# An attention and FFN block on one core: VectorE's exp as one quadratic per octave, and 256-query sets

## The chip, the cores and the metric

The kernel runs on one core of a Trainium2 chip, in one launch. The metric is device time in microseconds, the median of several runs. The core has five engines with in-order queues of their own: TensorE (PE, its weight loads shown as PEld), VectorE (DVE), ScalarE (ACT), GpSimd (POOL, which does almost nothing here) and SyncE (SP), which issues the DMAs. They wait for each other by semaphores.

## The reference

One transformer block for 2048 tokens of width 512, bf16 in and out. `mod` is six vectors of 512 made from a conditioning vector; attention has 32 heads of 16.

```python
h = _layernorm(x) * (1 + ca) + sa
qkv = (h @ wqkv)                      # q, k, v: 32 heads of 16
p = _softmax(q @ k.T * 16 ** -0.5)    # per head, 2048 x 2048
x = x + ga * ((p @ v) @ wo)
h = _layernorm(x) * (1 + cb) + sb
x = x + gb * ((gelu(h @ w_gate) * (h @ w_up)) @ w_down)   # F = 1792
```

The exps of the softmax are 32 x 2048 x 2048, a million columns of 128.

## The kernel before

**Recording and planning.** The Python class `_Recorder` records every operation with the memory it reads and writes, works out the semaphore waits, and keeps an estimate of when each engine will be free. The scheduling loop `stream` (line 1218) asks these estimates which operation to put next. What it decides is the fixed order of each engine's instructions in the built program; on the chip nothing is decided any more. Every matmul is issued from line 315, every ACT operation from line 328, DVE operations from lines 332 (two tensors), 340 (tensor and scalars), 345 (multiply-add of both), 349 (copy or cast), 352 (reciprocal) and 368 and 371 (layer norm statistics).

**The stream.** Queries are split into sets (`SETS`, line 31): three of 512, one of 256, two of 128. For each set there are eight units, one for each of eight groups `qd` of four heads, called head groups here. A unit walks over all keys in rounds; a round is four items (one for each of the four heads), and an item is one PSUM bank of 512 columns of scores: 128 keys x 512 queries, or 256 keys x 256 queries, or 512 x 128. The loop of `stream` takes items in *chunks* of three banks; there are two such triples, so while ACT works on one, PE fills the other (`qk`, line 1479). ACT takes the exp of a whole chunk in one instruction, from `ps_sc` to the buffer `E`. `pv_mms` (line 1491) then multiplies a round of `E` with V into the unit's accumulator `ps_pv`; V has a 17th column of ones that gives the softmax's denominator. The first two units are interleaved while K and V are still being projected.

**Exps on DVE.** In some chunks ACT takes two of the banks and DVE the third: it writes `score * a + b`, rounded to uint16, into a quarter of `kq` (tiles named `dreg` and `mreg` in the trace). Read as bf16, these bits are a power of two with a linear mantissa, a piecewise linear exp. After four such banks, a whole round (a *quad* in the code), DVE makes four copies of the 2048 columns with the bits shifted by the constants of `SHIFT` (line 60; `shift_task`, line 1503; in the trace `mreg<-dreg` and `mreg<-mreg` 128x2048). PV takes the five versions one after the other, the shifted ones with copies of V scaled by `2 ** (-shift / 128)` (`vs`), so that the five linear pieces add up to a closer exp. The scaled V exists for keys from tile `T0` = 12 on, so only such rounds may go to DVE. A new quad is begun only under conditions (lines 1394 to 1396): DVE not far behind, a backlog under `BACK`, a free `kq` buffer, and, once the third set's units are over, a low PE `credit` (PE's allowance for side work).

**Side work.** Projections, and for each finished set the output projection (`side_wo`), the second layer norm (`ln2_steps`) and the FFN (`side_ffn`), are generators whose matmuls are put between the chunks by the credits of `plan` (line 1144); they use the one bank `ps_mi`. A set's side work runs while the next set's attention does. `FLOW` sets stream gate, up and down weights anew, 256 KB a transfer, into `wst` and `wdst`; the later sets use weights that `weight_parts` loads once. gelu is made with a tanh on ACT (`wreg<-wreg`) and four DVE operations. A unit's end (`unit_end`, line 1525) copies the accumulator to `osb`, sends the denominators by DMA to other partitions, takes the reciprocal, sends it back broadcast to `rb` and multiplies. For the last two head groups (6 and 7) of the last two sets this is done without DMA by `near_end` (line 947): an fp32 matmul with `self32` spreads the denominators, DVE takes the reciprocal and the product.

**The tail.** After the last exp, `tail` (line 1580) orders what is left: the last set's (queries 1920 to 2047) wo, layer norm and FFN (`tail_end`, `tail_last`), and what is left of the FFN of the set before it (`tail_rest`). The last set but one is queries 1792 to 1919.

**Filler.** PE gets matmuls without use (`ps_sc<-xs,ident` and `ps_mi<-xs,ident`) when it would be idle for long.

Of the kernel before, what the change touches and what calls it, by code (L numbers as in the profile page):

```python
# [6 lines left out]
ALU = mybir.AluOpType  # L7
# [23 lines left out]
SETS = ((0, 512), (512, 512), (1024, 512), (1536, 256), (1792, 128), (1920, 128))  # L31
OCOL = (0, 0, 0, 0, 256, 384)
BCOL = (0, 0, 0, 0, 0, 128)
# [7 lines left out]
T0 = 12  # L41
NK = 3
CREDIT = 2048
NS = 4
AHEAD = (30, 44)
FLOW = 3
# [4 lines left out]
BACK = 8  # L51
# [8 lines left out]
SHIFT = (26, 51, 77, 102)  # L60
SHIFT_C = float(128 * (127 - np.log2(5) - 0.0565))
# [359 lines left out]
class _Kernel(_Recorder):  # L421
# [12 lines left out]
    def alloc(self):  # L434
# [9 lines left out]
        self.tb2 = hreg[:, 0:4 * D].rearrange("p (t n) -> p t n", t=4)  # L444
# [5 lines left out]
        self.wst = [[mreg[:, 1024 * (2 * x + b):1024 * (2 * x + b) + 1024].rearrange("p (a n) -> p a n", a=NDC)  # L450
                     for b in range(2)] for x in range(2)]
# [9 lines left out]
        self.wu = [self.wst[i // 2][i % 2] for i in range(4)]  # L461
        self.wu += [dreg[:, 1024 * i:1024 * i + 1024].rearrange("p (a n) -> p a n", a=NDC) for i in range(4, 7)]
# [3 lines left out]
        self.vs = sb("vs", [P, len(SHIFT), NKT - T0, H * VW], BF16)  # L466
# [245 lines left out]
    def side_v(self, g, dc):  # L712
        mi = self.mi[:, :]

        def part(t):
            for dci in range(NDC):
                self.mm(mi[:, P * t:P * t + P], self.hT[:, dci, 512 * g + P * t:512 * g + P * t + P],
                        self.wqkv[:, dci, 1024 + P * dc:1024 + P * dc + P],
                        start=(dci == 0), stop=(dci == NDC - 1))
        for t in range(4):  # L720
            yield 512, lambda t=t: part(t)
        dst = self.vaug[:, 4 * g:4 * g + 4, VW * 8 * dc:VW * 8 * dc + VW * 8]
        self.copy("dve", dst.rearrange("p t (h c) -> p t h c", c=VW)[:, :, :, 0:DH],
                  mi.rearrange("p (t h c) -> p t h c", t=4, c=DH))
        self.done(("v", g, dc))
        if 4 * g == T0 and not self.dry:
            c = slice(VW * 8 * dc, VW * 8 * dc + VW * 8)
            self.task([lambda i=i, o=o: self.ts("dve", self.vs[:, i, :, c], self.vaug[:, T0:NKT, c], float(2.0 ** (-o / 128)),
                                                None, ALU.mult) for i, o in enumerate(SHIFT)], ("vs", dc))
        yield END  # L730
# [155 lines left out]
    def normed(self, k, i):  # L886
        return self.E[:, NSL - 1, :] if k == len(SETS) - 1 else self.tb2[:, i, :]

    def merged(self, gi):
        return MERGED[gi >= len(SETS) - 2]  # L890
# [91 lines left out]
    def side_ffn(self, gi, part=None):  # L982
# [10 lines left out]
        width = max(2, kpb)  # L993
        for a in range(0, NFC, width):
            chunks.append(range(a, min(NFC, a + width)))

        def load(x, ci):
            if flow and ci < len(chunks):
                v = (self.B_w_gate, self.B_w_up)[x].rearrange("(a p) n -> p a n", p=P)
                self.dma("sp", self.wst[x][ci % 2], v[:, :, 2 * P * ci:2 * P * ci + 2 * P], "st%d%d" % (x, ci % 2))  # L1000
# [12 lines left out]
        for h in range(2):  # L1013
            yield from self.side_t(lambda t: self.normed(gi, t), n, h,
                                   lambda dc: self.t2T[:, dc, c0:c0 + W], self.modB)

        def up(x, ci, sub):
            for s, fc in enumerate(sub):
                for dci in range(NDC):
                    if flow:  # L1020
                        lhs = self.wst[x][ci % 2][:, dci, P * (fc % 2):P * (fc % 2) + P]
# [43 lines left out]
        for i in range(3):  # L1065
            load_down(i)
        for ci in range(nch + 1):
            yield from near()
            if ci < nch:
                yield from G(ci)  # L1070
                yield from near()
                if ci >= nch - 2:
                    load_down(3 + ci - nch + 2)
            if ci >= 1:
                yield from U(ci - 1)
                if ci >= nch - 1:
                    load_down(5 + ci - nch + 1)
# [21 lines left out]
    def urgency(self, tk):  # L1099

        if tk[1] is not None and tk[1][0] in ("rec", "norm", "onorm", "stats", "rstd", "den") or tk[1] in ((("ln2", len(SETS) - 1, h) for h in range(2))):
# [3 lines left out]
        if tk[1] is None or tk[1][0] in ("st2", "ln2"):  # L1105
            return -1
        if tk[1] is None or tk[1][0] != "shift":
            return 1
        return 0 if self.plain[tk[1][1]] <= URGENT else 2
# [34 lines left out]
    def plan(self, ends, nsplit):  # L1144
# [15 lines left out]
        due = (ends[1] + 30, ends[2] + 30, ends[3] + 30, ends[4] - 20)  # L1160
        for k, e in enumerate(due):
            s0 = ends[k] + 33
            w.append((lambda k=k: self.side_wo(k), s0, min(e, s0 + 15 * SETS[k][1] // P)))
            w.append((lambda k=k: self.side_ffn(k), s0, e))
        k, s0 = len(SETS) - 2, ends[-2] - 16
# [52 lines left out]
    def stream(self):  # L1218
# [7 lines left out]
        units = [((k,), qd) + SETS[k] for k in range(4) for qd in range(8)]  # L1226
        units += [((4, 5), qd, SETS[4][0], 2 * P) for qd in range(QS)]
        units += [((k,), qd) + SETS[k] for k in (4, 5) for qd in range(QS, 8)]
# [3 lines left out]
        ends = [0] * len(SETS)  # L1232
# [13 lines left out]
        for u in units[2:]:  # L1246
            n, kpb = NKT * u[3] // 512, 512 // u[3]
            plain = list(range(T0 // kpb))
            m = len(plain) * 2 // 3
            for r in plain[:m] + list(range(len(plain), n)) + plain[m:]:  # L1250
# [13 lines left out]
        for u, r, g0 in rounds:  # L1264
# [7 lines left out]
        cand = [k for k, (u, r, g0) in enumerate(rounds)  # L1272
                if u not in units[:2] and r * (512 // u[3]) >= T0]
# [60 lines left out]
        def pv_do(x):  # L1334
# [10 lines left out]
            else:  # L1345
                q["ready"].remove((i, src))
                q["n"] -= 1
                if i:
                    self.sq_free.append(q["slots"].pop(i))
# [9 lines left out]
        while cg <= group[units[-1]]:  # L1359
            parts = early or late  # L1360
            if parts and pos >= loaded and (pos >= ends[2] + 8 if early else ("ffn", 2) in self.have):
# [15 lines left out]
            if tq is not None and tq <= t + 30:  # L1377
# [9 lines left out]
                if len(mem) == CH and "modB" in self.have and self.free["dve"] < t + 700:  # L1387
                    while quad is None and cand and last[rounds[cand[0]][0]] < pos + AHEAD[rounds[cand[0]][0][3] == 512]:
# [5 lines left out]
                    elif (not overdue and cand and self.quad_free and (pos < ends[2] or self.credit < CREDIT or (self.next_side() is None and self.waiting[0] in ("onorm", "osb"))) and rounds[cand[0]][2] < pos + 96 and self.backlog() < BACK  # L1394
                          and ("vs", rounds[cand[0]][0][1] // 2) in self.have
                          and all(k in self.have for k in self.keys(seq[rounds[cand[0]][2]]))):
                        rnd = rounds[cand.pop(0)]
                        quad = {"rnd": rnd, "j": [0, 1, 2, 3], "k": self.quad_free.pop(0), "ready": [], "n": NS + 1, "slots": {}}
                        left[rnd[0]] += NS
# [24 lines left out]
                if g is not None:  # L1424
                    kq = self.kq[quad["k"]]
                    self.ts("dve", kq[:, 512 * j:512 * j + 512].bitcast(U16), self.scp[:, s0 + n, :], 128 / OCT, SHIFT_C,
                            ALU.mult, ALU.add)
                    if not quad["j"]:
                        quad["ready"].append((0, [kq[:, 512 * x:512 * x + 512] for x in range(4)]))
                        wait.append(quad)  # L1430
                        for i in range(NS):
                            self.shift_task(quad, i)
# [39 lines left out]
        self.tail(len(SETS) - 2, len(SETS) - 1)  # L1472
# [18 lines left out]
    def pv_mms(self, rnd, acc, src, i, first, last):  # L1491
# [3 lines left out]
        for kk in range(kpb):  # L1495
            kt = r * kpb + kk
            v = self.vs[:, i - 1, kt - T0, :] if i else self.vaug[:, kt, :]
            for j in range(4):
                h = 8 * dc + 2 * j + ee
                self.mm(acc[32 * j:32 * j + VW, 0:W], v[:, VW * h:VW * h + VW], src[j][:, W * kk:W * kk + W],  # L1500
                        start=first and kk == 0, stop=last and kk == kpb - 1, tp=(0, 32 * j))

    def shift_task(self, q, i):

        def f():
            s = self.sq_free[0]
            self.ts("dve", self.sq[s].bitcast(U16), self.kq[q["k"]].bitcast(U16), float(SHIFT[i]), None, ALU.add)
            if self.probing is None:
                self.sq_free.pop(0)
                q["slots"][i + 1] = s  # L1510
                q["ready"].append((i + 1, [self.sq[s][:, 512 * x:512 * x + 512] for x in range(4)]))
        self.task([f], ("shift", q["rnd"][0]), lambda: bool(self.sq_free))
# [12 lines left out]
    def unit_end(self, u, acc):  # L1525
# [5 lines left out]
        if sets[0] >= len(SETS) - 2 and len(sets) == 1 and qd >= 6:  # L1531
# [134 lines left out]
    def tail_rest(self, k, down):  # L1666
        if self.dry:
            return
        yield from self.until("last")
        q0, W = SETS[k]  # L1670
# [18 lines left out]
        yield from self.until("tail")  # L1689
        for fc in range(chunks[0][0]):  # L1690
# [99 lines left out]
```

## Time and profile before

| | |
|---|---|
| median of 3 runs | 849.17 us (849.08 to 849.26) |
| span of the profiled execution, first to last instruction | 847.7 us |
| granted TensorE clock | 1.000 |
| busy: ACT, PE, DVE, POOL | 823.6, 772.4, 715.3, 4.5 us |
| ACT exps over 3 banks and over 2 | 356 and 336 |
| DVE exps over 1 bank, shifts over 4 banks | 308 and 308 |
| DMA | 38.70 MB, 46 GB/s on average |

The profile is of one execution; the median is over others, and is 1.5 us above its span. Busy time is the time in which an engine has at least one of its instructions in work. A group's line has the operation, the tiles written and read, the form (partitions x elements), the count, the busy time, the mean of one, and the idle time ahead with what ended it. The chain follows the work that ended last back in time.

### The profile page before, as it was taken

Reading aid. Unit: us, or ns where it says so; the run is one execution under the profiler, and the core shown is the slowest. Engines: PE = TensorE matmul, PEld = TensorE weight load, DVE = VectorE, ACT = ScalarE, POOL = GpSimd, SP = SyncE. Lnnn points to the kernel's source line nnn. Section 1 sums busy time; section 2 is a strip of 40 time slices with the busy share of each in tenths; the row PEclk is TensorE's granted clock in tenths of the full one; section 3 lists DMA queues with packets and bytes.
Section 4 is the critical chain, followed back from the end, with each engine's and each line's share of the span. In section 5 each row is a group of like instructions: output and inputs, shape, how many; then the busy total and the mean of one; then the engine's idle time right before and its main releaser. Section 6 shows DMA issues by size and latency. Waiting matters only on the chain.

```text
span 847.7 us, 27698 instructions
## 1 busy us (share of the span) xinstructions
PE 772.4 (91%) x12435; PEld 278.1 (33%) x12437; DVE 715.3 (84%) x1387; ACT 823.6 (97%) x747; POOL 4.5 (1%) x12
## 2 busy tenths in 40 slices
PE   8899998988899899999998999899998889988888
PEld 3333332322222222222222222222333333335557
DVE  7855899989989998999999999999998778477475
ACT  7999999999999999999999999999999999999992
POOL 1000000000000000000000000000000000000000
PEclk9999999999999999999999999999999999999999
DMA  9100000000002111120002121110133222050000
GB/s 309 35 14 16 6 9 12 10 9 12 9 8 82 43 46 49 33 58 24 9 19 78 38 56 48 35 52 17 47 93 109 60 67 84 25 153 11 15 13 14
DMA packets 65368, 38.70 MB, mean 46 GB/s; under 512 B 18017, under 2 KB 63202, under 8 KB 65250
## 3 DMA queue, kind: packets, MB, share of 16 engines
q1 hardware_dynamic: 64720, 36.41, 15.7%
q8 instruction: 97, 1.59, 0.8%
q10 hardware_dynamic: 530, 0.53, 0.2%
q14 instruction: 21, 0.17, 0.1%
HBM read 33.56 MB, written 2.35 MB: 42 GB/s over the span
## 4 chain that ended last, share of the span: by engine, by line
ACT 91%; PE 6%; DVE 2%; DMA 1%; issue 0%; SPq 0%; DVEq 0%
ACT E L328 88%; ACT wreg L328 3%; PE ps_sc L315 2%; PE ps_mi L315 2%; PE ps_pv L315 1%; DMA den<-osb 1%; DMA xs<-in_A_x_dram 0%; DVE st L368 0%; DVE nwt L332 0%; DVE vaug L349 0%; DVE dreg L340 0%; DVE xs L332 0%; DVE rstd L345 0%; ACT dreg L328 0%; DVE mv L371 0%
## 5 line engine op out<-in xcount | busy, mean ns | idle before, releaser
L328 ACT ACTIVATE E<-ps_sc 128x1536 bf16<-128x1536 f32 (+2 forms) x698 | 797.1, 1381 | 10.5 <-PE ps_sc L315 10.5
L315 PE MATMUL ps_sc<-qT,kmo 32*128 32x512 bf16 (+2 forms) x1408 | 170.6, 323 | 20.3 <-ACT E L328 17.7
L315 PE MATMUL ps_sc<-qT,kme 32*128 32x512 bf16 (+2 forms) x1408 | 166.9, 323 | 19.7 <-ACT E L328 17.0
L315 PE MATMUL ps_pv<-E,vaug 128*17 128x512 bf16 (+2 forms) x2388 | 171.3, 318 | 4.3 <-ACT E L328 1.4
L340 DVE TENSOR_SCALAR dreg<-ps_sc 128x512 uint16<-128x512 f32 x208 | 143.1, 689 | 30.5 <-PE ps_sc L315 26.9
L340 DVE TENSOR_SCALAR mreg<-dreg 128x2048 uint16<-128x2048 uint16 x208 | 136.1, 681 | 0.2 <-PE ps_pv L315 0.2
L315 PE MATMUL ps_mi<-wreg,mreg 128*32 128x512 bf16 (+2 forms) x1504 | 112.8, 370 | 10.2 <-DVE wreg L345 6.4
L315 PE MATMUL ps_pv<-mreg,vs 128*17 128x512 bf16 (+2 forms) x1456 | 108.9, 347 | 0.8 <-DVE mreg L340 0.6
L315 PEld LDWEIGHTS ps_sc<-qT,kme 32*128 32x128 bf16 x1408 | 45.4, 91 | 142.5 <-ACT E L328 116.7
L315 PEld LDWEIGHTS ps_sc<-qT,kmo 32*128 32x128 bf16 x1408 | 45.9, 91 | 138.2 <-ACT E L328 119.1
L315 PEld LDWEIGHTS ps_pv<-E,vaug 128*17 128x17 bf16 x2388 | 52.9, 89 | 83.8 <-issue 54.4
L340 DVE TENSOR_SCALAR mreg<-ps_sc 128x512 uint16<-128x512 f32 x100 | 68.7, 689 | 11.1 <-PE ps_sc L315 9.5
L340 DVE TENSOR_SCALAR mreg<-mreg 128x2048 uint16<-128x2048 uint16 x100 | 66.7, 679 | 1.1 <-PE ps_pv L315 1.1
L315 PEld LDWEIGHTS ps_mi<-wreg,mreg 128*32 128x32 bf16 (+1 forms) x1504 | 34.1, 95 | 57.0 <-issue 19.7
L349 DVE CAST wreg<-ps_mi 128x512 bf16<-128x512 f32 x51 | 35.0, 685 | 11.9 <-PE ps_mi L315 11.6
L345 DVE SCALAR_TENSOR_TENSOR wreg<-wreg,ps_mi 128x512 bf16<-128x512 bf16 x51 | 34.8, 683 | 11.9 <-ACT wreg L328 6.1
L315 PEld LDWEIGHTS ps_pv<-mreg,vs 128*17 128x17 bf16 x1456 | 33.4, 89 | 30.9 <-DVE mreg L340 14.6
L315 PE MATMUL ps_mi<-hreg,wreg 128*32 128x512 bf16 (+1 forms) x496 | 40.4, 377 | 0.9 <-DVE vaug L349 0.8
L332 DVE TENSOR_TENSOR wreg<-wreg 128x1024 bf16<-128x1024 bf16 (+1 forms) x60 | 35.6, 602 | 0.4
L315 PE MATMUL ps_mi<-mreg,hreg 128*32 128x512 bf16 x384 | 33.5, 384 | 0.0
L328 ACT ACTIVATE wreg<-wreg 128x1024 bf16<-128x1024 bf16 (+1 forms) x30 | 32.0, 1071 | 0.8 <-DVE wreg L332 0.8
L315 PE MATMUL ps_sc<-xs,ident 128*32 128x512 bf16 x256 | 22.1, 385 | 8.4 <-ACT E L328 8.0
(149 smaller groups left out, 562.3 us busy)
## 6 DMA issues: line engine op xcount, KB each, us to landing
mreg<-in_B_w_up_dram SPq DMA_DIRECT2D x25, 256.0 KB, 3.3
mreg<-in_B_w_gate_dram SPq DMA_DIRECT2D x21, 256.0 KB, 3.2
rb<-scr_rec SPq DMA_DIRECT2D x96, 32.0 KB, 1.9
mreg<-in_B_w_down_dram SPq DMA_DIRECT2D x12, 256.0 KB, 2.8
dreg<-in_B_w_down_dram SPq DMA_DIRECT2D x9, 256.0 KB, 3.2
mreg<-in_w_mod_dram SPq DMA_DIRECT2D x1, 2048.0 KB, 12.6
out_dram<-xs SPq DMA_DIRECT2D x15, 128.0 KB, 1.7
xs<-in_A_x_dram SPq DMA_DIRECT2D x3, 512.0 KB, 6.5
```

What stands on the lines that cost most here:

```text
L315: return self.rec("pe", lambda e: e.matmul(out, lhsT, rhs, start=start, stop=stop, tile_position=tp), [lhsT, rhs], [out], cost=(n, int(rhs ...
L328: return self.rec("act", lambda e: e.activation(out, in_, func, scale=scale, **kw), rd, wr, cost=self.cost("act", out, [in_], "act"))
L332: return self.rec(eng, lambda e: e.tensor_tensor(out, a, b, op), [a, b], [out], cost=self.cost(eng, out, [a, b], "tt"))
L340: return self.rec(eng, lambda e: e.tensor_scalar(out, a, s1, s2, **kw), rd, [out], cost=self.cost(eng, out, [a], "ts") + (60 if len(rd) > ...
L345: return self.rec("dve", lambda e: e.scalar_tensor_tensor(out, a, s, b, op0=op0, op1=op1), rd, [out], cost=self.cost("dve", out, [a, b], " ...
L349: return self.rec(eng, lambda e: e.tensor_copy(out, in_), [in_], [out], cost=self.cost(eng, out, [in_], "ts"))
```

## The change

The set list becomes one set of 512 queries, five of 256 and two of 128; five sets instead of three stream their FFN weights (the streaming buffers get a tensor of their own, `freg`, and hold up to four 128-column blocks, 512 KB).

On DVE, the first operation stays, with another constant: linear in the exponent bits, into `kq`. Then three operations over the 2048 columns follow in place of four shifts: the mantissa bits alone with the exponent of a half (`(kq & 0x7F) | 0x3F00`, into `sq`), the product of `kq` and that (in place, bf16: the quadratic part), and the exponent bits of `kq` alone with the lowest bit set (`(kq & 0xFF80) | 1`, in place). PV takes the product and the masked `kq`, two passes, both with the unscaled V. `vs` and its 16 scalings go, and with them the restriction to keys from tile 12 on; any round after the first two units may go to DVE. The conditions for a new quad are loosened (`CREDIT` 2048 to 3500, DVE's lead in time, the third set replaced by the last streaming set) and `BACK` goes from 8 to 6, `NS` from 4 to 3. Due times in `plan` are spread by set size, gelu steps get a higher urgency, the loads of the down weights are spread over the gate chunks.

```diff
-SETS = ((0, 512), (512, 512), (1024, 512), (1536, 256), (1792, 128), (1920, 128))
+SETS = ((0, 512), (512, 256), (768, 256), (1024, 256), (1280, 256), (1536, 256), (1792, 128), (1920, 128))
-CREDIT = 2048
-NS = 4
+CREDIT = 3500
+NS = 3
-FLOW = 3
+FLOW = sum(a + n <= 1536 for a, n in SETS)
-BACK = 8
+BACK = 6
-SHIFT = (26, 51, 77, 102)
-SHIFT_C = float(128 * (127 - np.log2(5) - 0.0565))
+EXP_C = float(128 * (127 - np.log2(1.507027)))
+MANT, HALF, EXPO = 0x7F, 0x3F00, 0xFF80
...
-                if len(mem) == CH and "modB" in self.have and self.free["dve"] < t + 700:
+                if len(mem) == CH and "modB" in self.have and self.free["dve"] < max(t + 700, self.free["act"] + 150):
...
-            v = self.vs[:, i - 1, kt - T0, :] if i else self.vaug[:, kt, :]
...
-    def shift_task(self, q, i):
-
-        def f():
-            s = self.sq_free[0]
-            self.ts("dve", self.sq[s].bitcast(U16), self.kq[q["k"]].bitcast(U16), float(SHIFT[i]), None, ALU.add)
...
+    def square_task(self, q):
...
+        def mantissa():
+            self.ts("dve", self.sq[slot()].bitcast(U16), kq.bitcast(U16), MANT, HALF, ALU.bitwise_and, ALU.bitwise_or)
...
+        def square():
+            sq = self.sq[q["slot"]]
+            self.tt("dve", sq, kq, sq, ALU.mult)
...
+        def octave():
+            self.ts("dve", kq.bitcast(U16), kq.bitcast(U16), EXPO, 1, ALU.bitwise_and, ALU.bitwise_or)
...
+        self.task([mantissa, square, octave], ("shift", q["rnd"][0]), lambda: q["slot"] is not None or bool(self.sq_free))
...
+        yield from self.until(("t2T", k))
...
+        yield from self.until(("part", k))
```

More of the change, by code (lines that the diff above doesn't have):

```diff
@@ L1064, in side_ffn @@
         nch = len(chunks) if part is None else part
-        for i in range(3):
-            load_down(i)
+        down = list(range(7))
         for ci in range(nch + 1):
@@ L1099, in urgency @@
     def urgency(self, tk):
-        if tk[1] is not None and tk[1][0] in ("rec", "norm", "onorm", "stats", "rstd", "den") or tk[1] in ((("ln2", len(SETS) - 1, h) for h in range(2))):
+        if tk[1] is not None and tk[1][0] in ("rec", "norm", "onorm", "stats", "rstd", "den") or tk[1] in ((("ln2", NSETS - 1, h) for h in range(2))):
             return -3
@@ L1231, in stream @@
         rof = {}
-        ends = [0] * len(SETS)
+        ends = [0] * NSETS
         def add(u, r):
@@ L1246, in stream @@
         for u in units[2:]:
[L1247 to L1250, printed above, removed]
+            n = NKT * u[3] // 512
+            for r in range(n):
                 add(u, r)
@@ L1271, in stream @@
         self.sq_free = list(range(NS))
-        cand = [k for k, (u, r, g0) in enumerate(rounds)
-                if u not in units[:2] and r * (512 // u[3]) >= T0]
+        cand = [k for k, (u, r, g0) in enumerate(rounds) if u not in units[:2]]
         quad = None
@@ L1360, in stream @@
             parts = early or late
-            if parts and pos >= loaded and (pos >= ends[2] + 8 if early else ("ffn", 2) in self.have):
+            if parts and pos >= loaded and (pos >= ends[FLOW - 1] + 8 if early else
+                                            ("up" if len(late) > 4 else "ffn", FLOW - 1) in self.have):
                 parts.pop(0)()
```

100 lines of the change are left out of this document (52 added, 48 removed).

## The prediction, as it stood before the changed kernel was run

> **What bounds the kernel now.** I read the page's sums and chain first, then busy time by stage, then the chain in order of time, then the groups by form, and last the timeline after the last exp. The page:
>
> ```profile
> span 847.7 us, 27698 instructions
> PE 772.4 (91%) x12435; PEld 278.1 (33%) x12437; DVE 715.3 (84%) x1387; ACT 823.6 (97%) x747; POOL 4.5 (1%) x12
> ...
> ACT 91%; PE 6%; DVE 2%; DMA 1%; issue 0%; SPq 0%; DVEq 0%
> ```
>
> ACT is the chain for 91% of the span. By stage (window, its length, then PE, PEld, DVE, ACT busy):
>
> ```profile
> 480.00:560.00 80.00, 73.27 (x912) 20.33 (x912) 75.20 (x127) 80.00 (x75) 0.00 (x0) 1.00 0.17 44
> 640.00:720.00 80.00, 71.00 (x1356) 27.01 (x1352) 61.90 (x120) 80.00 (x66) 0.00 (x0) 1.00 0.29 79
> 760.00:800.00 40.00, 34.33 (x1104) 21.88 (x1100) 25.79 (x66) 39.29 (x34) 0.00 (x0) 1.00 0.09 22
> 820.00:848.00 28.00, 24.39 (x386) 19.48 (x386) 16.82 (x44) 12.64 (x18) 0.00 (x0) 1.00 0.05 13
> ```
>
> ACT is full from 80 us on, but for 0.7 us near 764 and the last 22 us. DVE is at 94% in the middle and has room only from 640 us on, in the 256-query set. So two things set the time: how much ACT has to do, and how long the tail behind the last exp is. The chain in order of time prices ACT's work, start to start:
>
> ```profile
> 286.27 0.93 ACT wreg L328
> 287.20 0.92 ACT E L328
> ...
> 345.65 0.94 ACT wreg L328
> 346.59 1.34 ACT E L328
> ```
>
> One exp over two PSUM banks holds ACT for 0.92, one over three for 1.34, a 1024-wide tanh for 0.94 us. (The group view's means, 1176 and 1589 ns, overlap with the next instruction.)
>
> **Part 1: exps that leave ACT.** Both programs' listings have 692 ACT exp instructions in the stream. Before, 356 cover three banks and 336 two; after, 328 and 364. 28 more chunks give a bank to DVE, 84 rounds of four instead of 77. That is 28 x (1.34 - 0.92) = 11.8 us less; the tanhs change from 21 wide and 9 narrow to 22 and 7: +0.94 - 2 x 0.52 (0.94 less the exps' 0.42 for 512 columns) = -0.1. **ACT: -11.9 us**, all ahead of the last exp.
>
> **Part 2: does DVE keep up?** These rows price it:
>
> ```profile
> L340 DVE TENSOR_SCALAR dreg<-ps_sc 128x512 uint16<-128x512 f32 x208 | 143.1, 689 | 30.5 <-PE ps_sc L315 26.9
> L340 DVE TENSOR_SCALAR mreg<-dreg 128x2048 uint16<-128x2048 uint16 x208 | 136.1, 681 | 0.2 <-PE ps_pv L315 0.2
> L332 DVE TENSOR_TENSOR wreg<-wreg 128x1024 bf16<-128x1024 bf16 x42 | 28.2, 682 | 0.2
> ```
>
> Out go 308 shifts at 0.681 (209.8 us) and 16 scalings of V (4.6). In come 28 more exps at 0.689 (19.3), 168 bitwise passes over 2048 and 84 products over 2048. Neither of the last two forms is in the trace. The nearest row to a bitwise pass is the shift itself, an immediate operation on the same uint16 tile: 0.681; its other end is a pass at one element per cycle, 2.26 (the f32 products of 256 and 512 columns, 419 and 682 ns, give 1.03 ns an element; 0.682 + 1536 x 1.03). I take 0.681: 114.4 us. A bf16 product takes 417 ns at 512 and 682 at 1024, so 0.682 + 2 x 0.265 = 1.21 at 2048 (ends: 0.68 as a shift, 2.26); 84 make 101.8. Shorter unit ends and layer norms add some 12 (32 more copies, products and reciprocals of 256 queries for 16 of 512, LN steps on more, smaller sets). DVE: -214 + 248 = +33, to about 749 of 844 us, 89%. Summed along the listing in stretches of 40 us of ACT work, start to start, DVE's work is 0.76 to 0.95 of ACT's after; before it was 0.81 to 0.96 until 650 us, with ACT full. So the 28 chunks fit, and they come from the end, where DVE had room: I cost DVE at nothing, its cover being 5% of ACT at the tightest.
>
> [...] No row here shows a bitwise pass, and the shift's row speaks for the fast rate only.
>
> **Part 3: PE.** PV rounds fall from 435 + 5 x 77 = 820 to 428 + 2 x 84 = 596. Full-array matmuls of 512 columns come 0.215 us apart (ten in 2.32 at 832.21, the last one's 0.17 latency off); four narrow ones run abreast, so 224 x 0.215 = 48 us go. Against it stand 65 filler groups (14 us, put where PE idles) and twice the instructions for the same columns: 16 matmuls of 128 columns take 0.40 us at 818.11, four abreast at full rate, so narrow passes cost columns, not instructions. PE waited, it did not bound; the relief is worth the 0.7 us stall at 764 at most: **-0.7**.
>
> **Part 4: SP and DMA.** 138 more issues and some 11 MB more weights on queues that are 16% busy; a 256 KB load lands in 3.3 us, a chunk ahead of its use. DVE's waits for rb (4.4 us in 6) may double, off the chain. Nothing; without that cover 4 us.
>
> **Part 5: the tail.** This is where the listing speaks against the change. Call T the end of the last exp, 817.35 + 8.22 = 825.57.
>
> ```profile
> 813.68 0.69 DVE L332 TENSOR_TENSOR xs<-xs,ps_mi 128x512 bf16<-128x512 bf16 x1 [1.56 <-PE ps_mi L315]
> 817.25 0.41 DVE L340 TENSOR_SCALAR hreg<-xs,mv,rstd 128x512 bf16<-128x512 bf16 x1
> 817.35 8.22 ACT L328 ACTIVATE E<-ps_sc 128x1536 bf16<-128x1536 f32 x6
> ...
> 826.98 0.96 DVE L352 RECIPROCAL rb<-ps_sc 128x128 f32<-128x128 f32 x1
> 829.59 0.69 DVE L368 BATCH_NORM_STATS2 st<-ps_sc 128x6 f32<-128x512 f32 x1
> 833.59 0.99 DVE L340 TENSOR_SCALAR E<-ps_sc,mv,rstd 128x256 bf16<-128x256 f32 x2
> 835.54 1.07 PE L315 MATMUL ps_sc<-wreg,qT 128*128 128x128 bf16 x16
> 845.18 0.41 DVE L332 TENSOR_TENSOR xs<-xs,ps_pv 128x256 bf16<-128x256 bf16 x1
> ```
>
> Before, the last set but one (queries 1792 to 1919) gets its residual sum 11.9 us ahead of T and its normalised tile 8.3 ahead. After, its wo matmuls stand around the last two chunks' QK, so the sum comes about 2 us ahead of T, and its norm, transposes and whole FFN fall into the last set's chain. Step by step behind T:
> - One more PV pass (0.2), then copy, fp32 matmul and reciprocal as before: reciprocal of head group 7 done at T+2.6 (before: 2.4).
> - On DVE now: product, the other set's norm (0.41); transposes and modulation, 0.97 a half (as 818.22 to 819.19): T+5.2. Only then its bank is free for head group 6's fp32 matmul (0.49) and reciprocal (0.96), which before were done ahead of T: T+6.8. PE then has 16 up matmuls (0.94) ahead of three wo (0.65 + 0.17): the last set's statistics start at **T+8.8, before T+4.0: +4.8**.
> - From there to the norm, 4.0 before with three of the other set's operations between; after, ten (five products at 0.34, two multiply-adds and a cast at 0.6, two scalings at 0.2, start to start: 3.9; statistics and aggregate 0.9, the eight small steps 0.1 each between them): 5.6, **+1.6**.
> - Norm to the first FFN matmuls with all operands: 1.95 before; a multiply-add (0.69) and a product (0.43) stand between: **+1.0**.
> - The FFN: eight down matmuls of the other set (8 x 0.215) and the wait for its sum (0.69) stand in it, with three matmuls begun early: **+2.0**.
> Sum **+9.4**, from 22.1 to 31.5 us.
>
> **Sum.** 847.7 - 11.9 - 0.7 + 9.4 = 844.5. The profiled span is 1.5 below the median of the runs, 849.17, which I take as what lies around it: **846.0 us**.
>
> **Rivals.**
> A. *The tail does not grow*: PE or DVE reach the other set's work early enough that its steps fill gaps. For: DVE and PE idle in the old tail (16.82 and 24.39 of 28). Against: the listing orders them in line. 847.7 - 11.9 - 0.7 + 1.5 = 836.6; part of it, 840.
> B. *Bitwise passes at one element a cycle*: 168 x 1.58 = 265 us more; DVE at 749 + 265 is the bound, about 1015 at 100% busy. Against: the shift row. [...]
> C. *The product in front of an exp* (the slower side). DVE runs in order, and the product is the first 1.21 us operation among 0.69s. A DVE exp may start late by 0.92 + 0.92 - 0.40 (QK) - 0.69 = 0.75 before its bank delays the chunk after next; behind a whole product it is 0.46 too late. 84 x 0.46 = 39 us at worst; it decides from (849.2 - 846.0) / 0.46 = 7 products on; 20 give 846.0 + 9 = 855. For: DVE at 0.95 of ACT in one stretch. Against: ACT was full at 0.96 before.
>
> **How the numbers follow.** Forecast 0.50, with 842 to 850 its own range (each tail step some 0.5 us uncertain, stalls that come and go some 2); A 0.22, C 0.22, B 0.06. 836.5 to 855 takes in A and most of C and leaves out B and C's far part. A measurement of this kernel tells 0.2% (1.7 us) from no change. Faster: A and 0.36 of the forecast's 0.50, 0.58. Same: 0.14 of it and 0.02 of C, 0.16. Slower: the rest, 0.26.
>
> **What would show it.** ACT's exp groups at 328 and 364 with 0.92 and 1.34 on the chain (part 1). The bitwise passes at 0.68 and products at 1.21 (part 2, B). ACT's waits ahead of the last exp under 3 us, and none on QK behind a late DVE exp (C). T near 813, and 31 us from T to the end, the last set's statistics near T+8.8 (part 5, A). The forecast is wrong if T is late, or the tail stays at 22.

## The result, and the profile after

The changed kernel takes **856.76 us** (median of 4 runs, 854.92 to 858.54) against 849.13 us of the kernel before (849.08 to 849.26): the ratio is 1.0086, 95% interval 1.0069 to 1.0103. It is slower by 0.9%. The forecast was 846.0, with a range from 836.5 to 855. The profiled execution took 854.92 us.

The page of the changed kernel, with the busy sums and the chain's shares by engine:

```profile
span 853.2 us, 32731 instructions
PE 749.3 (88%) x14847; PEld 321.2 (38%) x14851; DVE 742.4 (87%) x1411; ACT 813.0 (95%) x746; POOL 4.5 (1%) x12
...
ACT 81%; PE 8%; DVE 6%; DMA 3%; issue 1%; SPq 1%; DVEq 0%
```

ACT's busy time fell by 10.6 us, where 11.9 were forecast, but ACT is the chain for 81% of the span and no longer for 91%: PE, DVE and DMA now stand in the chain in its place. The groups by form show that the work itself is what was foretold:

```profile
L328 ACT ACTIVATE E<-ps_sc 128x1536 bf16<-128x1536 f32 x328 | 477.3, 1568 | 1.7 <-PE ps_sc L315 1.5
L328 ACT ACTIVATE E<-ps_sc 128x1024 bf16<-128x1024 f32 x364 | 370.1, 1151 | 6.2 <-PE ps_sc L315 6.0
...
L332 DVE TENSOR_TENSOR mreg<-dreg,mreg 128x2048 bf16<-128x2048 bf16 x56 | 68.1, 1216 | 0.1
L340 DVE TENSOR_SCALAR dreg<-dreg 128x2048 uint16<-128x2048 uint16 x56 | 38.2, 682 | 0.2
```

328 and 364 exps; a product takes 1.22 us, a bitwise pass 0.68. The idle column of the first two lines has grown: 7.9 us ahead of these exps, 7.5 of it waiting for QK (before: 2.9 and 2.8). By stage (window, length, PE, PEld, DVE, ACT, POOL busy, then the granted clock):

```profile
480.00:560.00 80.00, 70.62 (x1506) 31.42 (x1502) 70.00 (x130) 76.23 (x70) 0.00 (x0) 0.98 0.29 81
...
820.00:854.00 34.00, 24.55 (x330) 19.91 (x322) 18.25 (x55) 7.19 (x13) 0.00 (x0) 0.93 0.04 10
```

At 480 to 560 ACT lost 3.8 us (none before), and the clock fell to 0.98; from 820 on, in the tail, the clock is 0.93 and PE is busy for 24.6 of 34 us. So there are three places to look at: holes in the stream (gaps in which ACT has nothing to do), the tail, and the clock. T is again the end of the last exp of the stream. In the profiled execution before, T was 825.6 and the tail behind it 22.2 us; after, T is 820.0 and the tail 33.2. With 11.9 us less work for ACT, T should have come near 813.

**The largest hole**, in the timeline of the changed kernel:

```profile
486.67 0.58 SPq L378 DMA_DIRECT2D freg<-in_B_w_gate_dram  x1
...
490.96 0.35 PE L315 MATMUL ps_mi<-wreg,freg 128*32 128x256 bf16 x4 [1.88 <-DMA freg<-in_B_w_gate_dram]
491.24 0.39 PE L315 MATMUL ps_sc<-qT,kmo 32*128 32x256 bf16 x1
...
491.89 1.02 ACT L328 ACTIVATE E<-ps_sc 128x1024 bf16<-128x1024 f32 x1 [1.97 <-PE ps_sc L315]
```

A streamed set's first 512 KB of gate weights were asked for at 486.67. The first FFN matmuls, which read them, stood at the head of TensorE's queue for 1.88 us until they had landed; QK (`ps_sc<-qT`), which had all it needed, stood behind it; and ACT waited 1.97 us for QK. Another kind of hole needs no DMA:

```profile
278.82 0.68 DVE L340 TENSOR_SCALAR dreg<-ps_sc 128x512 uint16<-128x512 f32 x1
279.42 0.68 DVE L345 SCALAR_TENSOR_TENSOR wreg<-wreg,ps_mi 128x512 bf16<-128x512 bf16 x1
280.15 1.05 PE L315 MATMUL ps_mi<-wreg,freg 128*32 128x512 bf16 x16 [1.03 <-DVE wreg L345]
...
281.98 1.94 ACT L328 ACTIVATE E<-ps_sc 128x1024 bf16<-128x1024 f32 x2 [1.80 <-PE ps_sc L315]
```

16 FFN matmuls wait 1.03 us for a DVE step that empties the bank `ps_mi`, which itself came behind a DVE exp; then comes PV, which waits for DVE's copy of the accumulator (`osb`), and only then QK. All holes of over 50 ns between 100 us and T make 6.5 us in ten places; before, there was one of 0.7.

**The tail** in the same timeline (line 319 issues the transposes):

```profile
818.35 0.68 DVE L332 TENSOR_TENSOR xs<-xs,ps_mi 128x512 bf16<-128x512 bf16 x1
...
823.60 0.29 PE L319 MATMUL ps_mi<-ident,hreg 128*128 128x128 bf16 x2 [1.70 <-DVE hreg L340]
...
826.14 1.59 PE L315 MATMUL ps_sc<-wreg,qT 128*128 128x128 bf16 x13
...
827.53 1.27 PE L315 MATMUL ps_sc<-wreg,freg 128*128 128x128 bf16 x10
...
828.60 1.25 PE L315 MATMUL ps_mi<-wreg,qT 128*128 128x128 bf16 x16
...
830.53 0.70 DVE L368 BATCH_NORM_STATS2 st<-ps_sc 128x6 f32<-128x512 f32 x1
...
835.99 0.99 DVE L340 TENSOR_SCALAR E<-ps_sc,mv,rstd 128x256 bf16<-128x256 f32 x2
...
850.66 0.42 DVE L332 TENSOR_TENSOR xs<-xs,ps_pv 128x256 bf16<-128x256 bf16 x1
```

The residual sum of queries 1792 to 1919 comes 1.6 us ahead of T (before: 11.9), the last set's statistics at T+10.5 (before: 4.0), its norm at T+16.0.

### The profile page after: what moved, and what is told of

Its sections match the earlier page's. It is cut to its first block, busy times and chain, and to the rows that moved or that the text cites. A ratio compares the mean times of both kernels' runs of the same rounds, so it can differ in the third digit from the quotient of the medians.

```text
span 853.2 us, 32731 instructions
## 1 busy us (share of the span) xinstructions
PE 749.3 (88%) x14847; PEld 321.2 (38%) x14851; DVE 742.4 (87%) x1411; ACT 813.0 (95%) x746; POOL 4.5 (1%) x12
## 4 chain that ended last, share of the span: by engine, by line
ACT 81%; PE 8%; DVE 6%; DMA 3%; issue 1%; SPq 1%; DVEq 0%
ACT E L328 79%; PE ps_sc L315 3%; PE ps_mi L315 3%; ACT wreg L328 2%; PE ps_pv L315 2%; DMA scr_rec<-rden 1%; DVE wreg L345 1%; DMA rb<-scr_rec 1%; SPq L378 1%; DVE mreg L340 1%; DVE mreg L332 1%; DVE dreg L340 1%; DMA freg<-in_B_w_gate_dram 0%; DVE wreg L349 0%; DMA xs<-in_A_x_dram 0%
## 5 line engine op out<-in xcount | busy, mean ns | idle before, releaser
L328 ACT ACTIVATE E<-ps_sc 128x1024 bf16<-128x1024 f32 (+2 forms) x698 | 785.7, 1341 | 26.8 <-PE ps_sc L315 26.4
L315 PE MATMUL ps_sc<-qT,kme 32*128 32x256 bf16 (+2 forms) x1920 | 196.3, 281 | 23.4 <-ACT E L328 20.6
L315 PE MATMUL ps_sc<-qT,kmo 32*128 32x256 bf16 (+2 forms) x1920 | 194.0, 280 | 23.9 <-ACT E L328 22.1
L315 PE MATMUL ps_pv<-E,vaug 128*17 128x256 bf16 (+2 forms) x3116 | 173.7, 281 | 11.1 <-ACT E L328 6.5
L315 PE MATMUL ps_mi<-wreg,freg 128*32 128x256 bf16 (+2 forms) x2496 | 119.3, 295 | 14.4 <-DVE wreg L345 8.3
L315 PEld LDWEIGHTS ps_mi<-wreg,freg 128*32 128x32 bf16 (+1 forms) x2496 | 57.1, 96 | 53.2 <-issue 20.4
L332 DVE TENSOR_TENSOR mreg<-dreg,mreg 128x2048 bf16<-128x2048 bf16 x56 | 68.1, 1216 | 0.1
L315 PE MATMUL ps_sc<-xs,ident 128*32 128x512 bf16 x444 | 39.5, 385 | 14.4 <-ACT E L328 13.6
L315 PE MATMUL ps_pv<-mreg,vaug 128*17 128x256 bf16 (+2 forms) x880 | 42.9, 275 | 1.4 <-DVE osb L349 0.6
L340 DVE TENSOR_SCALAR dreg<-dreg 128x2048 uint16<-128x2048 uint16 x56 | 38.2, 682 | 0.2
L340 DVE TENSOR_SCALAR mreg<-dreg 128x2048 uint16<-128x2048 uint16 x56 | 38.1, 683 | 0.0
```

The source lines that it names most:

```text
L315: return self.rec("pe", lambda e: e.matmul(out, lhsT, rhs, start=start, stop=stop, tile_position=tp), [lhsT, rhs], [out], cost=(n, int(rhs ...
L328: return self.rec("act", lambda e: e.activation(out, in_, func, scale=scale, **kw), rd, wr, cost=self.cost("act", out, [in_], "act"))
L332: return self.rec(eng, lambda e: e.tensor_tensor(out, a, b, op), [a, b], [out], cost=self.cost(eng, out, [a, b], "tt"))
L340: return self.rec(eng, lambda e: e.tensor_scalar(out, a, s1, s2, **kw), rd, [out], cost=self.cost(eng, out, [a], "ts") + (60 if len(rd) > ...
```

## The experiments

Each kernel is the changed one with the edit shown. *Rounds* are those given to VectorE (84 after, 77 before); *holes* is ACT's idle time in gaps of over 50 ns between 100 us and T; *lead* is how far the residual sum of queries 1792 to 1919 lies ahead of T; the last four columns are of the profiled execution. A ratio is against runs of the kernel before that were made beside it.

| kernel | median us | ratio to before (95%) | rounds | T | holes | lead | tail |
|---|---|---|---|---|---|---|---|
| before | 849.1 | 1 | 77 | 825.6 | 0.7 | 11.9 | 22.2 |
| after | 856.8 | 1.0086 (1.0069 to 1.0103) | 84 | 820.0 | 6.5 | 1.6 | 33.2 |
| e1 old sets | 861.8 | 1.0147 (1.0114 to 1.0180) | 84 | 819.2 | 6.3 | -7.9 | 41.7 |
| e3 first loads early | 847.0 | 0.9969 (0.9956 to 0.9982) | 84 | 821.0 | 6.8 | 10.0 | 24.1 |
| e4 due time early | 850.7 | 1.0017 (1.0005 to 1.0029) | 84 | 824.1 | 10.6 | 10.6 | 24.1 |
| e5 both | 846.5 | 0.9960 (0.9944 to 0.9976) | 84 | 819.9 | 6.3 | 10.7 | 24.1 |
| e6 e5 + product halved | 850.0 | 1.0005 (0.9985 to 1.0024) | 83 | 823.2 | 8.3 | 10.3 | 25.2 |
| e7 e5 + more fillers | 856.0 | 1.0076 (1.0059 to 1.0093) | 84 | 826.1 | 9.0 | 4.5 | 27.9 |
| e8 e5 + old lead condition | 853.5 | 1.0066 (1.0041 to 1.0091) | 80 | 828.4 | 6.2 | 11.6 | 23.2 |
| e9 e1 + both edits | 862.8 | 1.0157 (1.0142 to 1.0172) | 84 | 819.5 | 5.8 | -7.9 | 41.8 |
| e10 ring of 15 | 852.6 | 1.0025 (1.0009 to 1.0041) | 84 | 825.0 | 10.3 | 5.7 | 26.2 |
| e11 e5 + ring of 15 | **839.7** | 0.9872 (0.9855 to 0.9888) | 84 | 813.1 | 0.8 | 10.5 | 23.1 |
| e12 before, 4250 | 858.7 | 1.0100 (1.0083 to 1.0117) | 75 | 835.6 | 3.6 | 16.5 | 21.3 |
| e13 after, 4250 | 849.9 | 1.0003 (0.9988 to 1.0018) | 84 | 824.0 | 8.5 | 10.4 | 23.3 |
| e14 e11, 4250 | 857.4 | 1.0090 (1.0070 to 1.0110) | 85 | 818.1 | 4.2 | -2.3 | 37.8 |
| e15 e5, 4250 | 851.3 | 1.0017 (1.0001 to 1.0034) | 84 | 823.1 | 7.9 | 9.9 | 25.4 |
| e16 e1, 4250 | 867.9 | 1.0216 (1.0195 to 1.0237) | 85 | 822.1 | 8.5 | -9.9 | 43.6 |

### Is it the exps, the sets, the first loads or a due time? (e1, e3, e4, e5)

e1 has the old `SETS` and `OCOL`. e3 asks for the next streamed set's first weights at the end of a set's up matmuls; e4 makes the FFN of queries 1536 to 1791 due earlier, and with it those of the sets between; e5 does both.

```diff
-        if flow:
+        if flow and gi == 0:
             load(0, 0)
             load(1, 0)
...
         if flow:
             self.done(("up", gi))
+        if gi + 1 < FLOW:
+            nw = min(1024 // SETS[gi + 1][1], 4) * P
+            for x in range(2):
+                v = (self.B_w_gate, self.B_w_up)[x].rearrange("(a p) n -> p a n", p=P)
+                self.dma("sp", self.wst[x][0][:, 0:NDC * nw].rearrange("p (a n) -> p a n", a=NDC), v[:, :, 0:nw], "st%d0" % x)
...
-            e = ends[m] - 20
+            e = ends[m] - 44
```

> The changed kernel with the query sets of the kernel before (512, 512, 512, 256, 128, 128), everything else as changed: the quadratic exps alone. Its ACT exps are the same, 328 over three banks and 364 over two. Theory S (the loss comes from the smaller query sets: weight loads with no cover, a later FFN ahead of the tail): the stream is full again and the last exp ends near 814, the tail is 22 to 25 us, time 837 to 841 us. Rival Q (the loss comes from the exps: the 1.22 us products on VectorE hold up exps and FFN steps): ACT stalls of 6 us in the stream as in the changed kernel, last exp near 820, a tail of 22 to 33 us, time 845 to 857 us.

> The changed kernel, with the first gate and up weights of the next streamed set loaded as soon as the set before it has done its up matmuls, not after its layer norm. Theory L (the stall at 490 us is the first 512 KB load, late by 1.9 us with QK queued behind it on TensorE, and the two gaps after it follow from it): ACT's gaps of 1.97, 0.49 and 0.36 us at 490 to 495 are gone, last exp near 817, time 853 to 855 us. Rival K (the granted clock falls there anyway): the gaps stay or move, time within 1 us of 856.8.

> The changed kernel with the due time of the FFN of queries 1536 to 1791 24 rounds' slots (some 9 us) earlier, which moves the due times of the sets between in proportion. Theory F (the tail grew because the FFN of queries 1536 to 1791 ends 10 us ahead of the last exp instead of 18, and holds the work of queries 1792 to 1919 behind it in the same list): its residual sum comes 9 us ahead of the last exp again, the last set's statistics at +4 to +6 us, tail 23 to 26 us, time 847 to 851 us. Rival H (queries 1792 to 1919 wait for their own last heads, or TensorE has no room for more work ahead of the last exp): tail 31 to 33 us as before, time 855 to 858 us.

> Both edits together: the first loads early and the due time 24 slots earlier. Theories L and F together: last exp near 817, tail 23 to 26 us, time 843 to 848 us, that is below the kernel before. Rivals K and H: 855 to 858 us. If only F holds 847 to 851, if only L holds 853 to 855.

**e1** refutes theory S: with the old sets, the exps and the planner's loosened conditions cost 12 us more than before, 5 more than the whole change. T is where rival Q put it, but the tail, 41.7 us, and the time are beyond both theories. Its timeline has the residual sum of queries 1792 to 1919 and the last set's statistics:

```profile
827.10 0.69 DVE L332 TENSOR_TENSOR xs<-xs,ps_mi 128x512 bf16<-128x512 bf16 x1 [1.24 <-PE ps_mi L315]
...
838.28 0.69 DVE L368 BATCH_NORM_STATS2 st<-ps_sc 128x6 f32<-128x512 f32 x1
```

T is 819.2: the sum comes 7.9 us behind it.

**e3**: theory L holds for the hole. The matmuls that had stood for 1.88 us have no wait ahead of them any more:

```profile
488.98 0.40 PE L315 MATMUL ps_mi<-wreg,freg 128*32 128x256 bf16 x8
```

The three gaps at 490 to 495 are gone. But T is not earlier (821.0): other holes, at 521 and 642 to 646 among them, came in their place, and the gain of 9.8 us, where 2 to 4 were expected, lies in the tail (9.1 us shorter). I had not foreseen that, and how it came about is not shown. The FFN of queries 1536 to 1791 has its first tanh 9 us sooner (763.5; 772.5 after the change), but the set ahead of it is 2 us later (673.0; 670.7), so the saved wait was not simply handed on from set to set.

**e4** came out as theory F said: lead 10.6, tail 24.1, 850.7 us, although T is 4 us later than after. That the due time did it is not shown: e3 has the same tail without it, and so has e13, below, by an edit that has nothing to do with the tail. e5, by the same lines as the tail above:

```profile
809.24 0.69 DVE L332 TENSOR_TENSOR xs<-xs,ps_mi 128x512 bf16<-128x512 bf16 x1 [0.19 <-PE ps_mi L315]
...
825.92 0.69 DVE L368 BATCH_NORM_STATS2 st<-ps_sc 128x6 f32<-128x512 f32 x1
```

With T at 819.9, the sum is at T-10.7 and the statistics are at T+6.0. Either edit gives a tail of 24.1, both together no shorter one, and e5 (846.5) is faster than the kernel before. The holes stay: 6.3 us, and T is not near 817 as expected.

Lead and tail go together: their sum is 32 to 36 us in all kernels of the table but e12 (37.8). The last instruction so follows the residual sum of queries 1792 to 1919 by some 34 us, wherever T lies. In e4 that sum is 4.8 us sooner than after, T 4.1 later, and the span 5.0 shorter.

### What makes the holes, and what makes the tail late with the old sets? (e6 to e9)

e6 splits the product in two halves, e7 sets `FILL` to 4600, e8 takes back the lead condition, e9 is e1 with both edits.

```diff
-        self.task([mantissa, square, octave], ...
+        self.task([mantissa, lambda: square(0), lambda: square(1), octave], ...
...
-FILL = 4200
+FILL = 4600
...
-                if len(mem) == CH and "modB" in self.have and self.free["dve"] < max(t + 700, self.free["act"] + 150):
+                if len(mem) == CH and "modB" in self.have and self.free["dve"] < t + 700:
```

> The kernel with both edits (first loads early, due time 24 slots earlier; 846.5 us), with VectorE's 2048-wide product done as two of 1024: no VectorE operation of the exps is then longer than 0.69 us. VectorE does 12 us more in all, and the plan gives it 83 rounds instead of 84, which puts 1.7 us back on ACT. Theory C (the stalls left in the stream, 1.80 us at 283, 0.82 at 472, 1.73 at 560, come from work behind a 1.22 us product): they go, 843 us. Rival P (they come from up matmuls that wait for a VectorE step in TensorE's order with QK behind them, whatever the length of one operation): stalls of some 5 us stay, 847 to 850 us.

> The kernel with both edits, with more filler matmuls on TensorE (the wanted columns in 3.4 us raised from 4200 to 4600; 97 more groups of four, 21 us of TensorE). Theory K (after a stall TensorE has idled, its granted clock falls, and that costs 2 to 3 us in the median run): the clock is 0.998 or more in every run, the times lie within 2 us of each other, median 843 to 845 us. Rival G (the clock is not what spreads the times, and the fillers take TensorE's room): spread of 5 us as before, median 846 to 850 us.

> The kernel with both edits, with the old condition for giving an exp to VectorE (only while VectorE's own queue reaches no more than 0.7 us ahead of TensorE's time; the change also allows it up to 0.15 us past ACT's). The plan then gives VectorE 80 rounds instead of 84: ACT has 16 chunks x 0.42 = 6.7 us more. Theory D (VectorE so full that FFN steps come late is what stalls ACT): the 5 us of stalls past 100 us go, 847 to 849 us. Rival E (the stalls have other causes): they stay, 852 to 854 us.

> The quadratic exps with the query sets of the kernel before (861.8 us, tail 41.7 us), with both edits: first loads early, due time 24 slots earlier. Theory F (the FFN of queries 1536 to 1791 is behind, since VectorE now does exps where it did FFN steps, and an earlier due time brings it back): tail 24 to 30 us, 843 to 850 us, about what the new sets give. Rival S' (sets of 512 queries leave the FFN behind whatever its due time, and the split into 256 is what the exps need): tail over 34 us, 855 to 862 us.

**e6**: theory C falls; with no DVE operation of an exp longer than 0.69 us the three holes named are gone, but others of 8.3 us in all stand in their place, and the time is 850.0 us. **e8**: theory D falls too; DVE has 17.5 us less to do (724.3 us busy against 741.8), the holes stay at 6.2, 853.5 us as rival E said. **e9**: rival S' stands; both edits leave the tail at 41.8. With sets of 512, the third set's FFN ends at 754 us (746 before), the last weights of the late sets are loaded behind it, and the first tanh for queries 1536 to 1791 is at 784 (768 before).

**e7** bears out half of theory K. In all four runs the clock was 0.998 or more, and they lie within 1.9 us. But the order that came with the fillers has 9.0 us of holes and a lead of 4.5, and the time is 856.0, above what either theory gave.

### Is it a ring that is full, or the order as it happened to be drawn? (e10 to e16)

The trace shows other holes at a unit's end, where PV waits for the copy of the one accumulator and QK stands behind PV: in the changed kernel PE waits 9 times for that copy, 2.8 us in all. `E` has 12 slots; e10 and e11 give it three more, in a part of `mreg` that the change left free. e12 to e16 change only the filler threshold from 4200 to 4250 columns. That adds some fillers and is not meant as a remedy; it makes the scheduling loop decide some steps otherwise, and with them all that follow. Such an order, one of many that the loop could have written, is called a *draw* below.

```diff
+RING = 15
...
-                e0 = 0 if e + len(mem) > NSL else e
+                e0 = NSL if e < NSL < e + len(mem) else e
+                if e0 + len(mem) > (RING if "modB" in self.have else NSL):
+                    e0 = 0
...
+        self.E2 = mreg[:, 10240:10240 + 512 * (RING - NSL)].rearrange("p (a n) -> p a n", n=512)
...
-FILL = 4200
+FILL = 4250
```

> The changed kernel (856.8 us) with three more slots of 512 columns for the exps that ACT has written and PV has not yet read: 15 in place of 12, the new ones in room that the change left free. Same rounds on VectorE (84), same work on every engine. Theory R (the stalls left in the stream are not VectorE's speed: a head group's end, where PV waits for the copy of the single accumulator, leaves the ring of 12 full, so that QK has to stand behind PV): the stalls of 1.8 us near 282 and 0.85 near 549 go; since the first loads and the due time are as they were, the one near 490 and a tail of some 26 to 33 us may stay; 848 to 854 us. Rival V (VectorE is late whatever the ring): stalls of 5 us or more past 100 us as before, 854 to 858 us.

> The kernel with both edits (first loads early, due time earlier; 846.5 us) and the 15 slots. Theory R: the 5 us of stalls past 100 us shrink to some 1 us, the last exp ends near 814 to 816, tail 24 us, 836 to 841 us. Rival V: 845 to 848 us.

> The kernel before, with the wanted columns of TensorE in 3.4 us at 4250 in place of 4200, an edit without a purpose: some more fillers, and an order drawn anew by the planner, with 75 rounds on VectorE in place of 77 (3.4 us of ACT). Theory O (each version's time is its work plus what the drawn order loses in stalls and tail, and that loss moves by several us at any edit): 855 to 859 us, most of it stalls and tail. Rival N (an order drawn anew costs what its work costs): 851 to 853 us.

> The changed kernel with the same edit, 4250 in place of 4200: 38 more groups of fillers, the same 84 rounds. Theory O: stalls elsewhere and another tail than 33 us, and a time that differs from 856.8 by over 2 us. Rival N: the same stalls and tail, 856 to 858 us. If the clock is most of what is lost, more fillers hold it and the time falls to 852 to 854 us with the stalls where they were.

> The kernel with both edits and the ring of 15 slots (839.7 us), its order drawn anew by 4250 wanted columns in place of 4200; 85 rounds on VectorE in place of 84 (1.7 us less ACT). Theory R (the ring takes the stalls away): stalls of under 2 us past 100 us again, 838 to 843 us, and 5 us or more below e15. Rival O (e11 was a lucky draw): stalls of 4 us and more, 844 to 852 us, within 3 us of e15.

> The kernel with both edits and the ring of 12 (846.5 us), its order drawn anew by the same edit. Theory R: stalls of some 5 us as in the draw before, 845 to 851 us. Rival O: 840 to 852 us, no worse than e14 on the mean of the two draws. In both the tail stays at 23 to 25 us if the two edits are what mended it.

> The quadratic exps on the old query sets (861.8 us, tail 41.7 us), drawn anew by the same edit; 85 rounds on VectorE. Theory S' (with sets of 512 queries the FFN ends too late for the tail in any order, so the exps need the smaller sets): tail over 34 us, 855 to 866 us. Rival O (the late FFN was that draw's): tail 22 to 28 us, 842 to 850 us.

**e11** was what theory R said: 839.7 us, T at 813.1, 0.8 us of holes, tail 23.1. It is the fastest kernel here, 1.3% below the kernel before. Its page and what ACT waited for (line numbers of the kernels with the ring are one higher):

```profile
span 836.2 us, 32715 instructions
...
PE 736.1 (88%) x14840; PEld 315.5 (38%) x14842; DVE 740.9 (89%) x1411; ACT 812.0 (97%) x746; POOL 4.5 (1%) x12
```

```profile
ACT E L329 <- PE ps_sc L316: 8.6, 10, 2.1
```

ACT and DVE do the same as after the change (812.0 and 813.0, 740.9 and 742.4), but ACT's exps and copies to `E` wait for PE for 8.6 us in 10 times, where the changed kernel has 26.4 in 15; 5.4 us of the difference are at exps of the stream, the rest is in the tail. **But the ring is not shown to be the reason.** e10, the ring alone, is in the time that theory R gave (852.6), and the holes near 282 and 549 shrank to 0.3 us or went, but it has 10.3 us of holes in all, as rival V said. The pair that was made to tell it apart went the other way: e14, with the ring, 857.4 us, above what either theory gave, e15, without, 851.3, just above theory R's range and inside rival O's. e14 has fewer holes (4.2; e15 7.9) and loses it all in a tail of 37.8 us, at a lead of -2.3, with both edits in it. In three pairs (e10 and after, e11 and e5, e14 and e15) the ring gave -4.2, -6.8 and +6.1 us. So e11 may be no more than a good draw. The residual sum and the statistics in the tails of e13 (first) and e14:

```profile
813.55 0.69 DVE L332 TENSOR_TENSOR xs<-xs,ps_mi 128x512 bf16<-128x512 bf16 x1
...
829.22 0.69 DVE L368 BATCH_NORM_STATS2 st<-ps_sc 128x6 f32<-128x512 f32 x1
```

```profile
820.38 0.68 DVE L333 TENSOR_TENSOR xs<-xs,ps_mi 128x512 bf16<-128x512 bf16 x1
...
832.36 0.69 DVE L369 BATCH_NORM_STATS2 st<-ps_sc 128x6 f32<-128x512 f32 x1
```


**e12** and **e13** show how large a draw is. The same purposeless edit made the kernel before 8.8 us slower, of which 8 chunks x 0.42 = 3.4 are ACT's work and 4.9 idle time of ACT (2.9 past 100 us, 2.0 ahead of it), and the changed kernel 6.9 us faster, with the same work on ACT and DVE. Each fell in the range of theory O. In e13 the tail went from 33.2 to 23.3 us, and the holes at 282 and 490 are gone, others (8.5 us) there instead. **e16** is what S' said of the tail, 43.6 us, in a second order; its time, 867.9, is above both ranges.

The other half of e1, the old exps on the new sets, was not tried, and so what the sets alone do is not known.

## Why the prediction was wrong

The step that failed is the count of ACT's idle time ahead of the last exp. The prediction took 0.7 us off for the one hole that there was (part 3), and put DVE's load (part 2) and the transfers (part 4) at nothing; the trace has 6.5 us of new holes, behind FFN matmuls at the head of TensorE's queue in the two that were read above.

It missed by 10.8 us: T came 7.0 late (820.0 for 813.0), the tail was 1.7 too long (33.2 for 31.5), what lies around the span was 1.7 instead of 1.5, and the median run is 1.8 above the profiled one.

**Part 1, right.** 328 and 364 exps, 22 and 7 tanhs. Where nothing is in the way, as in e11, T falls by 12.5 us.

**Part 2, right in its prices, wrong in "I cost DVE at nothing".** Bitwise pass 0.68, product 1.22 (taken: 1.21), DVE 742 us (taken: 749; of it, the 16 scalings of V at 4.6 us are a sum of means, they keep DVE busy for 3.6). Rival B is out: the trace has the bitwise passes over 2048 columns at 681 to 683 ns, the shifts before at 679 and 681. (The one element per cycle of its 2.26 us is a name for the 1.03 ns an element of the f32 products, 419 ns at 256 columns and 682 at 512.) DVE did keep up in the mean, and a fuller DVE did not make the holes (e8). But the room at the end had been used by FFN steps, and a DVE step that comes behind a DVE exp is part of the hole at 282. For queries 1536 to 1791 the first cast of a gate chunk is at 758.07 and its tanh at 772.47, 14.4 us; before, 762.65 and 768.49, 5.8 us (with chunks half as wide). In between, DVE now does eight exps and two operations over 2048 columns. That the 28 chunks must cost the lead does not follow: e13, with the same 84 rounds, has a lead of 10.4.

**Part 3, failed.** "The relief is worth the 0.7 us stall at 764 at most": I asked which holes would go and never which would come, but for "stalls that come and go some 2" in the range. 6.5 us came. (0.8 us of the idle time ahead of 100 us went, and the first exp is 0.2 us later. The other 1.2 us of T are busy time: up to T it fell by 10.7 us and not by 11.9. An exp with a hole behind it takes longer than the 0.92 us that were counted from start to start: 1.02 at 491.89.) The listing that I read has the order, but I took ACT as full because it was full before.

**Part 4, failed: "Nothing".** The transfer that mattered was not a later chunk, which is asked for a chunk ahead, but a set's first, which has no chunk ahead of it and is now 512 KB; by the chain, 4.25 us from issue to landing where I counted 3.3 and a cover. Its hole with the two behind it is 2.8 us (e3).

**Part 5, right in mechanism, mis-sized by 1.7.** The sum came at T-1.6 (said: 2), then statistics T+10.5 (8.8), 5.5 to the norm (5.6), 2.8 to the FFN (3.0), 14.4 to the end (14.1). Only the first term is off, and there the clock is, 0.50 from 825.58 to 828.99: at 826.14, 13 up matmuls of 128 columns take 1.59 us, 0.11 apart, twice the usual 0.06. They and the 26 behind them take 3.7 us, and at 0.06 apart would take 2.3, an estimate that leaves 1.4 of the 1.7 us to the clock. The table tells more than I knew: over 17 kernels the tail follows the lead, 21 to 25 us at a lead of about 10 or more, 26 to 28 at 5, 33 at 1.6, 38 to 44 below zero. So the change does not force the long tail: with the new sets and 84 rounds e13 has 23.3, and e3, e4, e5 and e11, edited, about as much, near rival A's. What makes an order early or late there is open.

**Rivals.** C named the price of the slow side, 855, by luck: its mechanism, the product's length, is not what makes the holes (e6), and the two that were read have FFN matmuls that wait at the head of TensorE's queue. A measured time inside the forecast's range would have been luck too: e13, at 849.9 us, has T at 824.0 for 813.0 and a tail of 23.3 for 31.5.

**The kernel as a whole.** Five designs were drawn twice by a purposeless edit: before 849 and 859, after 857 and 850, e1 862 and 868, e5 846 and 851, e11 840 and 857. The change's 12 us of ACT work are real; whether its orders lose more than those before, two draws each cannot tell. What stays open is why nearly all orders with the quadratic have 4 to 11 us of holes; product length, DVE's load, the set size and the ring were each tried and are not, alone, shown to be the reason. The planner's other new constants (`CREDIT`, `BACK`, the spread due times, the urgency of gelu) are in all these kernels and were not tried apart.

## What to carry to other kernels

Where a loop with a cost model writes out the order, an edit changes the work and also draws a new order: make a purposeless edit to both versions first, and see how far the draw alone moves them. Count new holes, not only old ones: look at the head of each in-order queue for an instruction whose operand has no cover (a first load, a step behind another engine's new work), and at what stands behind it. Read the tail from one number, how far ahead of the last exp the last but one set's work is done: an earlier last exp gains little where the end hangs on that work.

## What was not expected of the hardware

The forecast had no term for the granted clock, which was 1.000 in the profiled execution before; in the changed kernel it falls after TensorE waits of 1.88 and 1.70 us. Windows of 20 us in the changed kernel (clock behind POOL's count), and the tail of e7, with more fillers:

```profile
480.00:500.00 20.00, 16.19 (x323) 6.79 (x320) 15.86 (x36) 17.18 (x16) 0.00 (x0) 0.91 0.36 112
...
820.00:840.00 20.00, 14.45 (x205) 11.53 (x197) 14.31 (x48) 5.14 (x10) 0.00 (x0) 0.91 0.02 3
```

```profile
820.00:854.00 34.00, 27.34 (x462) 20.81 (x457) 19.93 (x59) 12.69 (x18) 0.00 (x0) 1.00 0.04 11
```

PE's longest waits in the two windows at 0.91 are 1.88 and 1.70 us; in the 20 us ahead of the first, where the longest is 0.7, the clock is 1.00. The clock record of the trace stands at 0.5 from 491.07 and from 825.58, for 3.41 us each. 3.41 us at a half in 20 us give a mean of 1 - 0.5 x 3.41 / 20 = 0.915, an estimate from that record; the rows have 0.91. What decides the fall is not shown: in e5 the clock is 0.91 from 180 to 200 us, with PE busy for 17.68 of the 20 us, and 1.00 from 200 to 220, with PE busy for 15.96. In runs of one kernel the time goes with the clock in part: e5's ten runs go from 843.5 us at a mean clock of 1.000 to 848.9 at 0.990; the kernel before stays within 0.994 to 1.000, and its runs go from 848.6 to 853.0, but at 1.000 alone they go up to 851.0.
